# One-hot rows of the list positions on GpSimd, and the scaling of the later lists' one-hot rows on GpSimd

## The chip, the cores and the metric

One core of a Trainium2 chip. The time is the device time of one execution in microseconds (us). Before the change the kernel takes 706.0 us, the median of three runs (705.8 to 706.21).

## What is computed

Two steps, all in fp32 accuracy.

1. Attention with a window, for 8 batches and 8 heads of dimension 64: 512 local tokens see the 32 global keys and the local keys within 32 positions; the 32 global tokens see all 544 keys.
2. A mixture of eight experts on the 8 x 544 = 4352 result rows of 512 features. The choice is "sticky": a token takes its own best expert, or keeps that of the token ahead of it.

```python
for b in range(B):
    prev_e = -1
    for s in range(S):
        fresh_e = int(np.argmax(logits[b, s]))
        if s == 0 or local_gate[b, s] < 0.5: e = fresh_e
        else: e = prev_e if prev_e >= 0 else fresh_e
        prev_e = e
        ...
        h = np.maximum(x[b, s] @ w1[e], 0.0)
        out[b, s] = p[e] * (h @ w2[e])
```

Which tokens an expert gets depends on the data, so the kernel must sort the tokens by expert while it runs, and it does that with one-hot matmuls.

## The kernel before

**Stages.** The attention runs over 48 units (per batch four pairs of heads for the local tokens, two for the global ones). TensorE makes scores, transposes and products; VectorE takes maxima and divides; ScalarE takes exponentials and copies out of PSUM; GpSimd copies q and k into padded layouts (`prep`, line 191, six pieces a unit, two buffers). The result rows go to a table `xs` in device memory. Then the expert part runs in blocks: three early blocks of 256 tokens (`early`), which use only the tokens of batches 0 to 4, then eight blocks of each expert's rest (`rem`, one of ten code paths by a count), then full blocks. Each block does mm1 (line 1251, 8 groups of 12 matmuls), the ReLU on ScalarE (1253) and its low part on VectorE (1254), mm2 (1262), and a store by an indirect DMA from GpSimd (1268). Weights come in fp32 and are split into a high and a low part: ScalarE casts (1150), VectorE subtracts (1160, 128 x 1024 from SBUF to SBUF).

**The sorting.** For each of the 34 columns of 128 tokens the rank of a token in its expert's list is split into a low part `plo` (0 to 127) and a high part `phi`. `low` (line 905) builds a one-hot of the low part, `o1[:, c, :]`, 128 wide for each token column; `pick` builds the one-hot of the high part against the wanted chunks (line 989), and from it two scaled copies: times the column number `t1` (991) and times the partition number (993). A matmul of both, summed over the columns (999), gives in PSUM for each list place the number of its token, and VectorE makes the index from it (1001, 1002). Three picks are made:

- *early lists* (columns 0 to 20, in the attention), for blocks 0 to 2;
- *first later list* (`lists`, all 34 columns, four chunks wide), for block 3. Before it `low` builds the last 13 columns. It is made in block 2's mm1, and block 3's four gathers wait for its index;
- *other later lists* (`rest`, 54 chunks wide, in four groups of 9, 9, 8 and 8 columns), for everything after block 3. It is made in block 2's mm2; its o2 lies in the space of the tile `xT`, so the profile calls it xT. Its matmuls come at the end of block 2.

**What sets the order.** Every engine works in the order in which the code was written; there is no scheduler. The routing is a generator of small steps. In the attention `drip` takes steps from it at fixed places (a step that yields HEAVY ends the turn at that place); in the expert blocks `hook`, which is called after each of 24 places of a block, takes one. `every(g, n)` lets n steps through at a time. In the last block of the early ones, tokens of block 3 are transposed after mm2 steps 2, 4, 5 and 6 (line 1205, two PSUM banks in turn), copied high by ScalarE (1207) and low by VectorE (1208), which frees the bank.

Of the kernel before, what the change touches and what calls it, by code (L numbers as in the profile page):

```python
# [8 lines left out]
F32 = mybir.dt.float32  # L9
F32R = mybir.dt.float32r  # L10
BF16 = mybir.dt.bfloat16
I32 = mybir.dt.int32
AF = mybir.ActivationFunctionType
ALU = mybir.AluOpType
# [4 lines left out]
P = 128  # L19
# [4 lines left out]
E = 8  # L24
# [6 lines left out]
NT = 34  # L31
# [7 lines left out]
NX = 3  # L39
LISTS = "lists"  # L40
KINDS = "kinds"
HEAVY = "heavy"
NF = (B * S) // 256
NR = NF - NX - 1
# [9 lines left out]
LATE = 99  # L54
# [14 lines left out]
def lag(n):  # L69
    for _ in range(n):  # L70
        yield
# [495 lines left out]
class Consts:  # L567
# [17 lines left out]
    def rest(self):  # L585
        v = self.idf.rearrange("p (h e) -> p e h", h=4)
        self.nc.vector.tensor_reduce(out=self.sel, in_=v[:, 0:9], axis=AX.X, op=ALU.add)


class Route:  # L590
# [4 lines left out]
    def setup(self):  # L595
        nc, cst, c = self.nc, self.cst, self.pool
# [31 lines left out]
        self.rv = c.tile([P, E, CA], F32, name="rv")  # L628
        self.pos = c.tile([P, NT], F32, name="pos")
        self.pi = c.tile([P, 2, NT], I32, name="pi")  # L630
        self.plo = c.tile([P, NT], BF16, name="plo")
        self.o1 = c.tile([P, NT, P], BF16, name="o1")
        self.oe = c.tile([P, CA, 2, 2 * NX], BF16, name="oe")
        self.idx = c.tile([P, 2 * NX + 4 * E + 2 * NR], I32, name="idx")
# [56 lines left out]
        for g in range(4):  # L691
# [17 lines left out]
                                in1=self.io8.rearrange("p (e o) -> p e o", o=1).broadcast_to([P, E, E]), op=ALU.is_equal)  # L709
# [191 lines left out]
        yield  # L901

    def low(self, c0, c1):
        b1 = [P, c1 - c0, P]
        self.nc.vector.tensor_tensor(out=self.o1[:, c0:c1], in0=self.io128.rearrange("p (o k) -> p o k", o=1).broadcast_to(b1),
                                     in1=self.plo[:, c0:c1].rearrange("p (t o) -> p t o", o=1).broadcast_to(b1), op=ALU.is_equal)
        yield HEAVY

    def place(self, cntp, n, k0, nk):
        nc = self.nc  # L910
# [66 lines left out]
        yield  # L977
        yield from self.pick(cid, phi, self.oe, 0, 2 * NX, 0, ((0, CA),), po)

    def pick(self, cid, phi, o2, c0, c1, i0, groups, po, wait=2):  # L980
        nc = self.nc
        w = c1 - c0
        ci = cid.rearrange("p (o s) j -> p o (s j)", o=1)
        last = groups[-1][1]
        for t0, t1 in groups:
            ts = slice(t0, t1)
            b2 = [P, t1 - t0, w]
            e = o2[:, ts, 1, c0:c1]
            nc.vector.tensor_tensor(out=e, in0=ci[:, :, c0:c1].broadcast_to(b2), in1=phi[:, ts].rearrange("p (t o) -> p t o", o=1).broadcast_to(b2), op=ALU.is_equal)  # L989
            yield  # L990
            nc.vector.tensor_tensor(out=o2[:, ts, 0, c0:c1], in0=e, in1=self.t1[:, ts].rearrange("p (t o) -> p t o", o=1).broadcast_to(b2), op=ALU.mult)  # L991
            yield
            nc.vector.tensor_scalar(out=e, in0=e, scalar1=self.ipf, scalar2=None, op0=ALU.mult)
            yield
        yield from lag(wait)
        yield PSUM
        lp = po()
        for t in range(last):
            nc.tensor.matmul(lp[:, 0:2 * w], self.o1[:, t], o2[:, t, :, c0:c1], start=(t == 0), stop=(t == last - 1))  # L999
        l1 = self.tmp("l1", [P, 4 * E + 2 * NR], F32)[:, 0:w]  # L1000
        nc.vector.tensor_scalar(out=l1, in0=lp[:, 0:w], scalar1=float(P), scalar2=None, op0=ALU.mult)
        nc.vector.tensor_tensor(out=self.idx[:, i0 + c0:i0 + c1], in0=l1, in1=lp[:, w:2 * w], op=ALU.add)
        yield
# [61 lines left out]
        yield  # L1065

    def rest(self, po):
        yield from self.pick(*self.pk, self.o2, 4, 2 * (2 * E + NR), 2 * NX, ((0, 9), (9, 18), (18, 26), (26, NT)), po, LATE)


class Moe:
# [497 lines left out]
```

## Time and profile before

| what | value |
|---|---|
| runs | 705.8, 706.0, 706.21 us |
| profiled execution | 705.68 us, of which the span from first to last instruction is 704.0 |
| TensorE busy | 673.2 us, 96% of the span |
| VectorE busy | 428.2 us, 61% |
| GpSimd busy | 197.7 us, 28% |
| mean granted TensorE clock | 0.985 |

The profile gives one execution. Its timeline rows hold the start in us from the span's start, the length, the engine (PE is TensorE, PEld its weight load, DVE VectorE, ACT ScalarE, POOL GpSimd, SP the queue of the plain DMAs), the line of the kernel, the operation, what it writes and reads, and, in brackets, how long the engine was idle before it and what ended that. An xN at the end joins N neighbours. The attention lasts until about 240 us, the three early blocks until about 326, with the two later picks from 291 to 327, and the remaining blocks until the end.

### The profile page before, as it was taken

Reading aid. Unit: us, or ns where it says so; the run is one execution under the profiler, and the core shown is the slowest. Engines: PE = TensorE matmul, PEld = TensorE weight load, DVE = VectorE, ACT = ScalarE, POOL = GpSimd, SP = SyncE. Lnnn points to the kernel's source line nnn. Section 1 sums busy time; section 2 is a strip of 40 time slices with the busy share of each in tenths; the row PEclk is TensorE's granted clock in tenths of the full one; section 3 lists DMA queues with packets and bytes.
Section 4 is the critical chain, followed back from the end, with each engine's and each line's share of the span. In section 5 each row is a group of like instructions: output and inputs, shape, how many; then the busy total and the mean of one; then the engine's idle time right before and its main releaser. Section 6 shows DMA issues by size and latency. Waiting matters only on the chain.

```text
span 704.0 us, 18381 instructions
## 1 busy us (share of the span) xinstructions
PE 673.2 (96%) x7253; PEld 564.2 (80%) x7253; DVE 428.2 (61%) x1057; ACT 343.3 (49%) x614; POOL 197.7 (28%) x321
## 2 busy tenths in 40 slices
PE   9999999999899899998998999999999999999991
PEld 7777777777677778887887988889988889899890
DVE  7878777777887787994516625335445325165551
ACT  4565555655355664652325635243535334256551
POOL 7634344243333311132022312040304020223312
PEclk9999999999999999999999999999999999999996
DMA  8966967865756487767319737255557245176561
GB/s 329 383 232 228 354 242 271 324 258 205 292 182 244 173 319 248 269 220 273 131 66 314 241 116 254 70 182 175 195 173 234 98 126 167 65 262 237 187 215 51
DMA packets 43011, 151.44 MB, mean 215 GB/s; under 512 B 7965, under 2 KB 9245, under 8 KB 38688
## 3 DMA queue, kind: packets, MB, share of 16 engines
q1 hardware_dynamic: 35536, 126.92, 50.5%
q0 software_dynamic: 6960, 21.90, 9.3%
q8 instruction: 77, 1.26, 0.7%
q14 instruction: 150, 1.23, 0.6%
q10 hardware_dynamic: 288, 0.13, 0.1%
HBM read 130.55 MB, written 19.69 MB: 213 GB/s over the span
## 4 chain that ended last, share of the span: by engine, by line
PE 59%; DVE 3%; issue 1%; ACT 0%; POOL 0%; DVEq 0%; POOLq 0%; ACTq 0%
PE ps L1262 28%; PE ps L1251 26%; PE ps L1205 3%; DVE wq L1160 1%; DVE wp L1160 0%; PE ps L1374 0%; DVE xT L991 0%; PE ps L999 0%; DVE xl L1160 0%; POOL xa L1191 0%; DVE xT L989 0%; DVE wp L1208 0%; PE ps L276 0%; DVE wq L1366 0%; DVE hh L1160 0%
## 5 line engine op out<-in xcount | busy, mean ns | idle before, releaser
L1268 POOL DMA_INDIRECT out_dram<-y,tk x39 | 40.7, 1042 | 317.9 <-ACT y L1267 297.8
L1262 PE MATMUL ps<-wp,wq 128*128 128x512 f32 x504 | 128.0, 401 | 0.9 <-ACT wq L1365 0.9
L1262 PEld LDWEIGHTS ps<-wp,wq 128*128 128x128 f32 x504 | 93.5, 190 | 20.6 <-ACT wq L1365 1.1
L1251 PE MATMUL ps<-wp,wp 128*128 128x256 f32 (+5 forms) x672 | 109.4, 323 | 0.0
L1251 PEld LDWEIGHTS ps<-wp,wp 128*128 128x128 f32 x672 | 103.8, 189 | 4.8
L1254 DVE SCALAR_TENSOR_TENSOR wq<-ps,wq 128x256 fp32r<-128x256 f32 (+5 forms) x80 | 41.7, 526 | 73.3 <-ACT wq L1253 70.7
L191 POOL TENSOR_SCALAR_AFFINE_SELECT qbd<-raw 64x512 f32<-64x512 f32 x62 | 44.6, 719 | 120.2 <-PE ps L243 100.8
L1208 DVE TENSOR_TENSOR wp<-ps,wp 128x512 fp32r<-128x512 f32 x40 | 27.5, 691 | 79.8 <-ACT wp L1207 79.8
L1253 ACT ACTIVATE wq<-ps 128x256 fp32r<-128x256 f32 (+5 forms) x80 | 37.2, 468 | 78.6 <-PE ps L1251 68.7
L243 PE MATMUL ps<-kx,qbd 128*64 128x128 f32 x1024 | 71.3, 281 | 1.8 <-issue 1.8
L1267 ACT ACTIVATE y<-ps,pp 128x512 f32<-128x512 f32 x39 | 26.9, 690 | 77.3 <-PE ps L1262 71.0
L243 PEld LDWEIGHTS ps<-kx,qbd 128*64 128x64 f32 x1024 | 55.2, 138 | 11.7 <-issue 7.6
L248 DVE TENSOR_REDUCE mx<-ps 128x4 f32<-128x512 f32 x64 | 43.9, 686 | 28.5 <-PE ps L243 28.3
L1160 DVE TENSOR_TENSOR wp<-raw,wp 128x1024 fp32r<-128x1024 f32 x47 | 57.0, 1217 | 2.9 <-ACT wp L1150 2.8
L1191 POOL DMA_INDIRECT xa<-xs,idx x42 | 52.2, 1242 | 17.1 <-issue 10.0
L254 ACT ACTIVATE pe<-pe 128x512 f32<-128x512 f32 x64 | 40.7, 636 | 32.3 <-DVE pe L250 32.3
L1150 ACT CAST wp<-raw 128x1024 fp32r<-128x1024 f32 x49 | 50.8, 1046 | 1.5 <-DMA raw<-in_w_dram 0.7
L1207 ACT CAST wp<-ps 128x512 fp32r<-128x512 f32 x40 | 23.5, 591 | 55.1 <-PE ps L1205 55.1
L250 DVE TENSOR_TENSOR pe<-ps,mx 128x512 f32<-128x512 f32 x64 | 44.1, 688 | 1.6
L276 PE MATMUL ps<-v,pt 128*32 128x65 f32 x2048 | 43.1, 224 | 1.6 <-ACT pe L254 0.6
L276 PEld LDWEIGHTS ps<-v,pt 128*32 128x32 f32 x2048 | 33.7, 111 | 13.1 <-issue 7.5
L191 POOL TENSOR_SCALAR_AFFINE_SELECT kx<-raw 128x384 f32<-128x384 f32 (+3 forms) x127 | 43.1, 372 | 2.9 <-DMA raw<-in_qk_dram 0.8
(279 smaller groups left out, 1172.4 us busy)
## 6 DMA issues: line engine op xcount, KB each, us to landing
raw<-in_w_dram SPq DMA_DIRECT2D x78, 512.0 KB, 3.8
v<-in_vw_dram SPq DMA_DIRECT2D x32, 1040.0 KB, 9.8
raw<-in_qk_dram SPq DMA_DIRECT2D x32, 528.0 KB, 9.4
xa<-in_w_dram SPq DMA_DIRECT2D x26, 512.0 KB, 4.7
xT<-in_w_dram SPq DMA_DIRECT2D x20, 512.0 KB, 4.2
xs<-xa SPq DMA_DIRECT2D x8, 1056.0 KB
qgb<-in_qg_dram SPq DMA_DIRECT2D x8, 128.0 KB
xa<-xs,idx POOLq DMA_INDIRECT x42
```

The lines of the kernel that those rows point to most:

```text
L191: self.nc.gpsimd.affine_select(out=out, in_=in_, pattern=pat, compare_op=ALU.is_ge, fill=0.0, base=0, channel_multiplier=0)
L243: nc.tensor.matmul(sp[64 * t2:64 * t2 + 64, t], qbd[:, w], kf[:, f:f + P], start=False, stop=True, skip_group_check=True)
L248: nc.vector.tensor_reduce(out=mx, in_=st["sp"], axis=AX.X, op=ALU.max)
L250: nc.vector.tensor_tensor(out=st["pe"][:, 4 * hb:4 * hb + 4], in0=st["sp"], in1=mx.broadcast_to([P, 4, P]), op=ALU.subtract)
L254: self.nc.scalar.activation(out=pe, in_=pe, func=AF.Exp, scale=SCALE)
L276: nc.tensor.matmul(o[32 * w4:32 * w4 + 32, g, h], pt[:, 2 * g + w4 // 2, w4 % 2, h, :], v[:, w, h * (D + 1):(h + 1) * (D + 1)], start=True ...
L1150: nc.scalar.copy(out=hi, in_=raw)
L1160: (nc.gpsimd if pool else nc.vector).tensor_tensor(out=lo, in0=raw, in1=hi.bitcast(F32), op=ALU.subtract)
L1191: self.nc.gpsimd.indirect_dma_start(out=self.xr[j] if k == "early" else self.xr4[:, j], out_offset=None, in_=src, in_offset=bass.IndirectO ...
L1251: nc.tensor.matmul(ph, a[:, dc, fs], b_[:, dc, n0:n1], start=(n == 0), stop=(n == 11))
L1254: nc.vector.scalar_tensor_tensor(out=hl[:, fc, n0:n1], in0=ph, scalar=0.0, in1=hh[:, fc, n0:n1].bitcast(F32), op0=ALU.max, op1=ALU.subtract)
L1262: nc.tensor.matmul(py, a[:, fc, js], b_[:, fs], start=(fc == 0 and k == 0), stop=(fc == 7 and k == 2))
```

## The change

`low` no longer builds three or five columns with one VectorE comparison, but one column after the other with a GpSimd `tensor_scalar`, which compares the row 0 to 127 with one number per partition. For that `plo` is held in fp32. Its step no longer ends the turn of `drip`. In `rest`, and there alone, the two scalings of `pick` go to GpSimd.

```diff
-        self.plo = c.tile([P, NT], BF16, name="plo")
+        self.plo = c.tile([P, NT], F32, name="plo")
...
     def low(self, c0, c1):
-        b1 = [P, c1 - c0, P]
-        self.nc.vector.tensor_tensor(out=self.o1[:, c0:c1], in0=self.io128.rearrange("p (o k) -> p o k", o=1).broadcast_to(b1),
-                                     in1=self.plo[:, c0:c1].rearrange("p (t o) -> p t o", o=1).broadcast_to(b1), op=ALU.is_equal)
-        yield HEAVY
+        for c in range(c0, c1):
+            self.nc.gpsimd.tensor_scalar(out=self.o1[:, c], in0=self.io128, scalar1=self.plo[:, c:c + 1], scalar2=None, op0=ALU.is_equal)
+        yield
...
-    def pick(self, cid, phi, o2, c0, c1, i0, groups, po, wait=2):
+    def pick(self, cid, phi, o2, c0, c1, i0, groups, po, wait=2, share=False):
...
-            nc.vector.tensor_tensor(out=o2[:, ts, 0, c0:c1], in0=e, in1=self.t1[:, ts].rearrange("p (t o) -> p t o", o=1).broadcast_to(b2), op=ALU.mult)
+            eng = nc.gpsimd if share else nc.vector
+            eng.tensor_tensor(out=o2[:, ts, 0, c0:c1], in0=e, in1=self.t1[:, ts].rearrange("p (t o) -> p t o", o=1).broadcast_to(b2), op=ALU.mult)
             yield
-            nc.vector.tensor_scalar(out=e, in0=e, scalar1=self.ipf, scalar2=None, op0=ALU.mult)
+            eng.tensor_scalar(out=e, in0=e, scalar1=self.ipf, scalar2=None, op0=ALU.mult)
             yield
...
     def rest(self, po):
-        yield from self.pick(*self.pk, self.o2, 4, 2 * (2 * E + NR), 2 * NX, ((0, 9), (9, 18), (18, 26), (26, NT)), po, LATE)
+        yield from self.pick(*self.pk, self.o2, 4, 2 * (2 * E + NR), 2 * NX, ((0, 9), (9, 18), (18, 26), (26, NT)), po, LATE, True)
```

The lines after `low` move up by one, so that line 989 of before is 988 in the changed kernel; 991, 993 and 999 keep their numbers.

GpSimd's instructions in the attention, where the early lists are made (o_290 is `o1`, io the row 0 to 127; kx and qbd are the padded k and q). Before:

```order
L191 AFFINE_SELECT kx_146<-raw_79 128x32
L191 AFFINE_SELECT kx_146<-raw_79 128x7x32
L191 AFFINE_SELECT qbd_145<-raw_80 64x16x32 x2
L191 AFFINE_SELECT kx_147<-raw_80 128x128
L191 AFFINE_SELECT kx_147<-raw_80 128x6x64
```

Now:

```order
L191 AFFINE_SELECT kx_146<-raw_79 128x32
L191 AFFINE_SELECT kx_146<-raw_79 128x7x32
L905 TENSOR_SCALAR o_290<-io_261,plo 128x128 x21
L191 AFFINE_SELECT qbd_145<-raw_80 64x16x32 x2
L191 AFFINE_SELECT kx_147<-raw_80 128x128
L191 AFFINE_SELECT kx_147<-raw_80 128x6x64
```

All 21 columns stand ahead of one preparation of q and k; the routing steps behind them come up to a unit earlier on VectorE.

GpSimd's instructions in the early blocks (the four stores are those of blocks 0 and 1, xa receives block 3's tokens, cnd are the counts that choose the code path). Before:

```order
L1268 DMA out_dram<-y_4316,tk_95 4352x512
L1268 DMA out_dram<-y_4317,tk_95 4352x512
L1268 DMA out_dram<-y_4318,tk_96 4352x512
L1268 DMA out_dram<-y_4316,tk_96 4352x512
L1191 DMA xa_108<-xs,idx 128x528 x4
L1434 TENSOR_LOAD cnd
```

Now:

```order
L1268 DMA out_dram<-y_4331,tk_95 4352x512
L905 TENSOR_SCALAR o_290<-io_261,plo 128x128 x13
L1268 DMA out_dram<-y_4332,tk_96 4352x512
L1268 DMA out_dram<-y_4330,tk_96 4352x512
L1191 DMA xa_108<-xs,idx 128x528 x4
L991 TENSOR_TENSOR xT<-xT,t_264 128x9x54
L993 TENSOR_SCALAR xT<-xT,ipf 128x9x54
L991 TENSOR_TENSOR xT<-xT,t_264 128x9x54
L993 TENSOR_SCALAR xT<-xT,ipf 128x9x54
L991 TENSOR_TENSOR xT<-xT,t_264 128x8x54
L993 TENSOR_SCALAR xT<-xT,ipf 128x8x54
L1434 TENSOR_LOAD cnd
```

The 13 columns stand between the stores of blocks 0 and 1, the scalings behind the gathers; the fourth pair comes behind the read of the counts.

VectorE's instructions in block 2's mm2, where the later lists are made. Before:

```order
L989 TENSOR_TENSOR xT<-cid,phi 128x9x54
L991 TENSOR_TENSOR xT<-xT,t_264 128x9x54
L993 TENSOR_SCALAR xT<-xT,ipf 128x9x54
L989 TENSOR_TENSOR xT<-cid,phi 128x9x54
L1160 TENSOR_TENSOR wp_4208<-raw_79,wp_4208 128x1024
L991 TENSOR_TENSOR xT<-xT,t_264 128x9x54
L993 TENSOR_SCALAR xT<-xT,ipf 128x9x54
L989 TENSOR_TENSOR xT<-cid,phi 128x8x54
```

Now:

```order
L988 TENSOR_TENSOR xT<-cid,phi 128x9x54 x2
L1160 TENSOR_TENSOR wp_4222<-raw_79,wp_4222 128x1024
L988 TENSOR_TENSOR xT<-cid,phi 128x8x54 x2
L1160 TENSOR_TENSOR wp_4326<-raw_80,wp_4326 128x1024
L1434 TENSOR_LOAD cnd
```

The eight scalings have left VectorE's queue; the weight subtractions (1160) follow the comparisons directly, and behind them stands the first L1208.

## The prediction

> **What bounds the kernel now.** I read the page first, then a table of stretches, then TensorE's and VectorE's timelines around the two places that the change touches.
>
> The page's first part (engine, busy time, share of the span, instructions) says that TensorE is the bound:
>
> ```profile
> PE 673.2 (96%) x7253; PEld 564.2 (80%) x7253; DVE 428.2 (61%) x1057; ACT 343.3 (49%) x614; POOL 197.7 (28%) x321
> ```
>
> VectorE at 61% would not matter on average, so the stretches decide. The table gives, for each, its length, then each engine's busy time, the granted TensorE clock, the DMA share and GB/s:
>
> ```profile
> 189.00:197.00 8.00, 6.39 (x94) 4.53 (x97) 4.76 (x21) 2.17 (x6) 2.79 (x6) 0.79 0.32 130
> 295.00:307.00 12.00, 12.00 (x126) 11.77 (x125) 10.87 (x27) 5.75 (x11) 5.72 (x5) 1.00 0.73 232
> 318.00:327.00 9.00, 6.84 (x54) 5.51 (x54) 5.46 (x11) 2.45 (x4) 1.00 (x1) 0.81 0.59 198
> ```
>
> From 295 to 307 TensorE is full and VectorE is busy 10.87 of 12 us: it follows at its heels. From 318 to 327 TensorE loses 2.16 us outright, and the clock stands at 0.81 (of 9 us, 0.19 x 9 = 1.7 us of work lost). TensorE's timeline (start, length, what, idle before and its releaser) shows why:
>
> ```profile
> 318.29 0.39 PE L1262 MATMUL ps<-wq,hl 128*128 128x512 f32 x1
> 320.84 1.03 PE L1205 MATMUL ps<-idf,xa 128*128 128x128 f32 x4 [2.16 <-DVE wp L1208]
> ```
>
> The third transpose of block 3's tokens waits for a PSUM bank that VectorE's first L1208 must empty, and that L1208 comes late because VectorE first works off the later lists:
>
> ```profile
> 309.44 0.64 DVE L989 TENSOR_TENSOR xT<-cid,phi 128x486 bf16<-128x486 bf16 x1
> 310.12 0.67 DVE L991 TENSOR_TENSOR xT<-xT,t 128x486 bf16<-128x486 bf16 x1
> 310.82 0.36 DVE L993 TENSOR_SCALAR xT<-xT,ipf 128x486 bf16<-128x486 bf16 x1
> ...
> 318.97 1.22 DVE L1160 TENSOR_TENSOR xl<-raw,xh 128x1024 fp32r<-128x1024 f32 x1
> 320.10 1.28 DVE L1208 TENSOR_TENSOR wp<-ps,wp 128x512 fp32r<-128x512 f32 x2
> ```
>
> **The question of the port.** Taking work from VectorE helps only if GpSimd can do it beside VectorE. These rows say that it can't (VectorE and GpSimd, two places):
>
> ```profile
> 231.88 2.97 DVE L740 TENSOR_TENSOR lvm<-sk,lvm 128x5 f32<-128x5 f32 x1
> ```
> ```profile
> 232.43 2.38 POOL L1160 TENSOR_TENSOR wp<-raw,wp 128x1024 fp32r<-128x1024 f32 x1
> ```
> ```profile
> 56.41 1.33 POOL L191 TENSOR_SCALAR_AFFINE_SELECT kx<-raw 128x128 f32<-128x128 f32 x4
> ```
> ```profile
> 203.05 1.52 POOL L191 TENSOR_SCALAR_AFFINE_SELECT kx<-raw 128x128 f32<-128x128 f32 x4
> ```
> ```profile
> 56.67 0.57 DVE L760 TENSOR_SCALAR lsu<-lsu 128x5 f32<-128x5 f32 x1
> ```
> ```profile
> 203.02 0.33 DVE L925 TENSOR_TENSOR hb<-oh,bs 128x168 f32<-128x168 bf16 x1
> ```
> ```profile
> L760 DVE TENSOR_SCALAR lsu<-lsu x8: 172/370/567, 56.7 to 271.2; 128x5 f32<-128x5 f32 x8
> ```
>
> L740 subtracts five columns and ends at 234.85, 0.04 us after GpSimd's subtraction. L760 takes 172 ns alone and 0.57 us when it starts in a run of four GpSimd pieces; it ends at 57.24, before the run does (57.74), so it got in between two pieces. The other way round, GpSimd's same run takes 1.52 us where L925, with both inputs in SBUF, stands at its start. So I treat them as one server for work from SBUF to SBUF: whoever is in finishes his instruction, then the one who waits goes. VectorE's operations on PSUM (L1254, L1208) I leave out of it. The Trainium skill (SBUF — State Buffer, Who interferes with whom) speaks against the change: a VectorE instruction with two SBUF inputs and a GpSimd instruction that reads SBUF exclude each other for the whole instruction. By that rule the sum is the one below, and without it the first rival's; the rows agree with it for L740 and L925, while for L1160 against GpSimd no row shows it.
>
> **Prices.** The trace has no compare and no scaling on GpSimd. The nearest rows (shape, count, total us, mean ns):
>
> ```profile
> L191 POOL TENSOR_SCALAR_AFFINE_SELECT kx<-raw 128x384 f32<-128x384 f32 x32 | 17.5, 547 | 0.0
> ...
> L191 POOL TENSOR_SCALAR_AFFINE_SELECT kx<-raw 128x128 f32<-128x128 f32 x32 | 9.9, 310 | 2.9 <-DMA raw<-in_qk_dram 0.8
> L191 POOL TENSOR_SCALAR_AFFINE_SELECT kx<-raw 128x32 f32<-128x32 f32 x32 | 6.8, 214 | 0.0
> ...
> L1160 POOL TENSOR_TENSOR wp<-raw,wp 128x1024 fp32r<-128x1024 f32 x2 | 4.8, 2378 | 4.4 <-DVE gx L774 4.4
> ```
>
> One column of 128 one-hots (one input): above 0.21 us (the 32-column piece), below 0.30 us (128 columns at the two-input rate of 2378/1024 = 2.32 ns). I take 0.28, a little under 0.31, since in the run at 56.41 the pieces overlap slightly. L991 (two inputs): 486 x 2.32 = 1.13 us and 1.00 for 432 columns, above; 486 x 547/384 = 0.69, below; I take 1.1 and 1.0, since the two-input row is the nearest in kind. L993 (one input): 214 + 454 x (547 - 214)/352 ns = 0.64 us, between 0.36 (VectorE's own) and 1.13.
>
> **The sum, part by part.**
>
> *Lists of the first half (attention).* VectorE loses seven L905, GpSimd gains 21 pieces:
>
> ```profile
> L905 DVE TENSOR_TENSOR o<-io,plo 128x384 bf16<-128x384 bf16 x8 | 4.4, 553 | 0.0
> ```
> ```profile
> 190.96 1.51 POOL L191 TENSOR_SCALAR_AFFINE_SELECT qbd<-raw 64x512 f32<-64x512 f32 x2 [8.45 <-PE ps L243]
> ```
> ```profile
> 198.47 1.09 PE L243 MATMUL ps<-kx,qbd 128*64 128x128 f32 x16
> ...
> 205.10 0.44 PE L352 MATMUL ps<-idf,xa 128*128 128x128 f32 x2 [0.79 <-DVE xa L284]
> ```
>
> 21 x 0.28 = 5.9 us goes ahead of one preparation of q and k, in a GpSimd idle time of 8.45 us, and that preparation is first read at 198.47: hidden, and even at 0.30 it ends some 5 us early. VectorE's 7 x 0.55 = 3.9 us come out while TensorE is full; the routing steps that moved up fill the same slots earlier. At best the wait of 0.79 us on VectorE goes; at worst it comes back elsewhere with a piece of blocking. I take **-0.3** (-1.1 to +0.5).
>
> *Lists of the second half.* This is where the port bites. VectorE's timeline, and the matmuls on TensorE that read the one-hots:
>
> ```profile
> 291.41 1.22 DVE L1160 TENSOR_TENSOR wp<-raw,wp 128x1024 fp32r<-128x1024 f32 x1
> ...
> 292.74 1.55 DVE L905 TENSOR_TENSOR o<-io,plo 128x640 bf16<-128x640 bf16 x2
> 294.21 1.22 DVE L1160 TENSOR_TENSOR wq<-raw,wq 128x1024 fp32r<-128x1024 f32 x1
> 295.34 0.55 DVE L905 TENSOR_TENSOR o<-io,plo 128x384 bf16<-128x384 bf16 x1
> 295.81 0.29 DVE L989 TENSOR_TENSOR xT<-cid,phi 128x136 bf16<-128x136 bf16 x1
> ...
> 300.06 0.75 DVE L1254 SCALAR_TENSOR_TENSOR hl<-ps,hh 128x256 fp32r<-128x256 f32 x2
> ```
> ```profile
> 298.05 1.01 PE L999 MATMUL ps<-xT,o 128*128 128x8 bf16 x34
> ```
>
> Today the one-hots are built at 292.74 and 295.34 and L999 finds them ready at 298.05. Now 13 pieces start at 291.45; behind them on GpSimd stands only the store of block 1's first half, and its y is one of three buffers, not written again until block 2. Between 291.41 and the first L1254 VectorE still has ten SBUF operations (five L1160, L1029, L1031, L989, L991, L993): without L905, 8.65 - 1.47 - 0.47 = 6.7 us. If each lets one piece in, L1254 starts at 291.41 + 6.7 + 10 x 0.28 = 300.9, and only then, on operations that read PSUM, do the last three pieces run through: 301.8. L999 needs the last column; it ends at 302.0 instead of 299.06: **+3.0** (at 0.21 us: 2.2; pieces that all run first end at 295.1, but then L1254, at 300.06 - 1.94 + 3.64 = 301.8, holds up the fourth L1251 group by over 1 us). Behind L999 the index, the gathers and everything on TensorE move with it. Such a gap also lowers the clock: after the gaps at 189 and 318 the stretches stand at 0.79 and 0.81, 1.7 us each. Here TensorE still trickles; I add **+1.0** (0 to 1.7).
>
> *Later lists.* From the first L989 to the first L1208 VectorE now needs 320.10 - 309.44 = 10.66 us. Without the scaling it needs 4 x 0.60 + 4 x 1.13 + 0.1 = 7.0. But GpSimd's pieces come between its L1160 and L989: three L991 and three L993 by the time of L1208, some of the last one beside VectorE's read of the counts, 1.1 + 0.64 + 1.1 + 0.64 + 0.6 + 0.6 = 4.7. Sum 11.7, **+0.8** after the 0.2 us by which VectorE had lagged (-3.7 without any blocking, +2 with L993 at 1.13). The last pair ends about 1.5 us after L1208, when TensorE, at 2 x (0.44 + 0.7) us of transposes and matmuls, just gets to L999: hidden; with slower pieces it becomes the next wait.
>
> Sum: -0.3 + 3.0 + 1.0 + 0.8 = **+4.5 us**. The profiled execution took 705.68, so 710.2; the runs' median is 0.3 above it, so **710.5**.
>
> **Rivals.**
> 1. *The engines don't exclude each other here* (the bf16 operations or L1160 escape). Then the pieces are ready at 295.1, VectorE needs 7.0 us instead of 10.66, and the wait of 2.16 us goes with its slow clock: -0.3 - 2.2 - 1.7 = -4.2, **701.8**. For it: VectorE is the releaser at 320.84 and GpSimd is idle there. Against: the rows of the port. Chance 0.25.
> 2. *The pieces are so cheap that both places cancel*: no place in the rows goes that low. By the Trainium skill (GPSIMD Engine Reference, Performance versus the Vector engine) a one-input body runs at 1.03 cycles an element of 1.2 GHz, an estimate of 0.11 us a column and 0.42 for L993; then L999 waits some 0.5 us, VectorE's stretch hardly changes, and the time would be about 706.5. With pieces at half my price the same result follows from my schedule: 300.06 - 1.94 + 1.4 + 0.4 = 299.9, a wait of 0.9, against a gain of about 1.3 before L1208: **706**. Chance 0.08.
> 3. *Compare and scaling cost more than the copies* (0.45 us a column, scalings a third more): 13 pieces end at 304, the scalings after L1208: +8, **714**. Nothing in the trace excludes it. Chance 0.10.
> Forecast: 0.57; its own range 707.5 to 713.
>
> **How the numbers follow.** A difference under 0.2% (1.4 us) is no change. Forecast and third rival are slower: 0.67; the second is the same: 0.08; the first faster: 0.25. The range reaches down to the first rival with some gain in the attention, 700.5, and up to half of the third's, 713.5.
>
> **What would show it.** In the changed profile: L999 at about 298 with a wait for GpSimd of some 3 us, columns of 0.28 us stretched among VectorE's L1160; VectorE's L1160 above 1.22 us where a scaling precedes it; the third transpose still waiting for L1208. Wrong, if L1160 stays at 1.22 us beside running GpSimd pieces, if the 13 pieces end before 298, or if the 2.16 us wait has gone.

## The result and the profile after

The changed kernel takes 713.91 us (median of five runs, 711.45 to 715.45) against 706.0 for the kernel before (704.2 to 707.08 beside it): a ratio of 1.0109, with a 95% interval from 1.0088 to 1.0131. It is slower, as forecast, but by 7.7 us instead of 4.5, and just above the range (713.5). The profiled execution took 713.91 us, of which the span is 712.2. The page's first part says that TensorE still sets the time and that only GpSimd has more to do:

```profile
PE 676.8 (95%) x7253; PEld 566.5 (80%) x7253; DVE 420.6 (59%) x1039; ACT 343.1 (48%) x614; POOL 235.8 (33%) x363
```

GpSimd gained 235.8 - 197.7 = 38 us of busy time, VectorE lost 428.2 - 420.6 = 7.6. The 38 us are not all work: part of it is instructions that are counted as busy and don't get on. That shows where the 13 later columns stand. GpSimd's timeline of the changed kernel, column by column (start, length; the columns behind 297.63 are left out, each takes 0.59 us):

```profile
290.21 1.62 POOL L905 TENSOR_SCALAR o<-io,plo 128x128 bf16<-128x128 bf16 x1 [17.73 <-DVE cid L1026]
291.82 1.52 POOL L905 TENSOR_SCALAR o<-io,plo 128x128 bf16<-128x128 bf16 x1
293.33 0.65 POOL L905 TENSOR_SCALAR o<-io,plo 128x128 bf16<-128x128 bf16 x1
293.96 2.38 POOL L905 TENSOR_SCALAR o<-io,plo 128x128 bf16<-128x128 bf16 x1
296.32 1.33 POOL L905 TENSOR_SCALAR o<-io,plo 128x128 bf16<-128x128 bf16 x1
297.63 0.59 POOL L905 TENSOR_SCALAR o<-io,plo 128x128 bf16<-128x128 bf16 x1
...
```

VectorE in the same stretch:

```profile
290.10 1.22 DVE L1160 TENSOR_TENSOR wp<-raw,wp 128x1024 fp32r<-128x1024 f32 x1
...
291.53 1.21 DVE L1160 TENSOR_TENSOR wq<-raw,wq 128x1024 fp32r<-128x1024 f32 x1
...
293.50 2.45 DVE L1160 TENSOR_TENSOR wq<-raw,wq 128x1024 fp32r<-128x1024 f32 x2
295.87 1.30 DVE L1160 TENSOR_TENSOR wq<-xa,wq 128x1024 fp32r<-128x1024 f32 x1
```

A column costs 0.59 us when nothing is in its way (from 297.63 on). While VectorE works off its subtractions a column takes up to 2.38 us, and five are done by 297.65; the other eight come after VectorE's row has ended. VectorE pays little: a subtraction takes 1.21 to 1.30 us where it took 1.22 before. TensorE then waits for each of the last nine columns, and its clock falls (TensorE's timeline, then the table of stretches: length, busy time of PE, PEld, DVE, ACT and POOL, granted clock, DMA share, GB/s):

```profile
296.73 0.79 PE L999 MATMUL ps<-xT,o 128*128 128x8 bf16 x25
297.70 0.18 PE L999 MATMUL ps<-xT,o 128*128 128x8 bf16 x1 [0.19 <-POOL o L905]
...
302.32 0.19 PE L999 MATMUL ps<-xT,o 128*128 128x8 bf16 x1 [0.39 <-POOL o L905]
```
```profile
302.50:307.50 5.00, 5.00 (x25) 5.00 (x25) 1.74 (x4) 0.38 (x1) 3.92 (x4) 0.50 0.44 134
```

L999 ends at 302.51 instead of 299.06, though TensorE came to it 1.3 us earlier (296.73 against 298.05), so some 4.8 us are lost in it, and the next 5 us run at half the clock: 2.5 us of work are lost there.

At the other later lists the wait of 2.16 us for L1208 has gone, and another has come. GpSimd's scalings, and TensorE's matmuls that read them:

```profile
315.27 6.93 POOL L991 TENSOR_TENSOR xT<-xT,t 128x486 bf16<-128x486 bf16 x1 [4.71 <-DVE xT L988]
322.30 1.53 POOL L993 TENSOR_SCALAR xT<-xT,ipf 128x486 bf16<-128x486 bf16 x1
323.81 0.99 POOL L991 TENSOR_TENSOR xT<-xT,t 128x486 bf16<-128x486 bf16 x1
...
329.72 1.37 POOL L993 TENSOR_SCALAR xT<-xT,ipf 128x432 bf16<-128x432 bf16 x1
```
```profile
326.16 1.03 PE L999 MATMUL ps<-xT,o 128*128 128x108 bf16 x18
328.80 0.54 PE L999 MATMUL ps<-xT,o 128*128 128x108 bf16 x8 [1.61 <-POOL xT L993]
331.14 0.65 PE L999 MATMUL ps<-xT,o 128*128 128x108 bf16 x8 [1.80 <-POOL xT L993]
```

VectorE's row there begins and ends so, and between these rows it has no gap:

```profile
314.54 1.22 DVE L988 TENSOR_TENSOR xT<-cid,phi 128x486 bf16<-128x486 bf16 x2
...
320.13 1.21 DVE L1160 TENSOR_TENSOR xl<-raw,xh 128x1024 fp32r<-128x1024 f32 x1
322.15 0.69 DVE L1208 TENSOR_TENSOR wp<-ps,wp 128x512 fp32r<-128x512 f32 x1 [0.81 <-ACT wp L1207]
```

The first scaling stands for 6.93 us where its like takes 0.99, and ends 0.9 us after VectorE's row (321.34). The first L1208 waits for ScalarE and is no longer late.

### The profile page after: what moved, and what is told of

The parts are those of the page before. It is cut to its first block, busy times and chain, and to the rows that moved or that the text cites. A ratio compares the mean times of both kernels' runs of the same rounds, so it can differ in the third digit from the quotient of the medians.

```text
span 712.2 us, 18411 instructions
## 1 busy us (share of the span) xinstructions
PE 676.8 (95%) x7253; PEld 566.5 (80%) x7253; DVE 420.6 (59%) x1039; ACT 343.1 (48%) x614; POOL 235.8 (33%) x363
## 4 chain that ended last, share of the span: by engine, by line
PE 57%; DVE 4%; POOL 2%; issue 1%; DMA 0%; ACT 0%; POOLq 0%; DVEq 0%; SPq 0%; ACTq 0%
PE ps L1262 28%; PE ps L1251 25%; PE ps L1205 2%; DVE wp L1160 1%; POOL o L905 1%; DVE wq L1160 1%; DMA raw<-in_w_dram 0%; PE ps L1374 0%; DVE hl L1254 0%; POOL xa L1191 0%; DVE xl L1208 0%; POOL xT L993 0%; DVE xl L1160 0%; PE ps L276 0%; DVE hl L1160 0%
## 5 line engine op out<-in xcount | busy, mean ns | idle before, releaser
L1268 POOL DMA_INDIRECT out_dram<-y,tk x39 | 39.0, 999 | 281.8 <-ACT y L1267 272.8
L1262 PEld LDWEIGHTS ps<-wp,wq 128*128 128x128 f32 x504 | 94.1, 191 | 21.3 <-ACT wq L1365 1.3
L1254 DVE SCALAR_TENSOR_TENSOR wq<-ps,wq 128x256 fp32r<-128x256 f32 (+5 forms) x80 | 41.8, 525 | 75.8 <-ACT wq L1253 61.6
L1208 DVE TENSOR_TENSOR wp<-ps,wp 128x512 fp32r<-128x512 f32 x40 | 27.5, 691 | 80.6 <-ACT wp L1207 80.5
L243 PEld LDWEIGHTS ps<-kx,qbd 128*64 128x64 f32 x1024 | 55.4, 138 | 12.2 <-issue 8.5
L1160 DVE TENSOR_TENSOR wp<-raw,wp 128x1024 fp32r<-128x1024 f32 x47 | 56.8, 1215 | 2.8 <-ACT wp L1150 2.8
L262 ACT COPY pt<-ps 128x512 f32<-128x512 f32 x64 | 34.9, 610 | 18.9 <-PE ps L260 15.1
```

The source lines that it names most:

```text
L243: nc.tensor.matmul(sp[64 * t2:64 * t2 + 64, t], qbd[:, w], kf[:, f:f + P], start=False, stop=True, skip_group_check=True)
L1160: (nc.gpsimd if pool else nc.vector).tensor_tensor(out=lo, in0=raw, in1=hi.bitcast(F32), op=ALU.subtract)
L1254: nc.vector.scalar_tensor_tensor(out=hl[:, fc, n0:n1], in0=ph, scalar=0.0, in1=hh[:, fc, n0:n1].bitcast(F32), op0=ALU.max, op1=ALU.subtract)
L1262: nc.tensor.matmul(py, a[:, fc, js], b_[:, fs], start=(fc == 0 and k == 0), stop=(fc == 7 and k == 2))
```

## The experiments

The theory after the first comparison, V in the expectations: while VectorE has operations with two SBUF inputs ready one behind the other, GpSimd is held off, and gets in only now and then; and GpSimd's form with a scalar per partition is dearer than I took it. Its rival, A, is what the prediction used: the two take turns, one GpSimd piece at each end of a VectorE operation. Others are named with the runs. In the kernels of the experiments lines are shifted by a few: a column is L907, the list's matmul L1006 (L1011 and L1010 in the later ones), the subtraction L1167 (L1172, L1171), the low part of the transposes L1215 (L1220, L1219). Each ratio is to the kernel before, run beside it.

### One part of the change at a time

First half alone: the flag `share` stays false, and `low` builds the later columns on VectorE as before.

```diff
     def low(self, c0, c1):
+        if c0 < CA:
             for c in range(c0, c1):
                 self.nc.gpsimd.tensor_scalar(out=self.o1[:, c], in0=self.io128, scalar1=self.plo[:, c:c + 1], ...)
             yield
+            return
+        ...  # the VectorE comparison of before, from a bf16 copy of plo
```

> Only the 21 columns of the first half (attention) go to GpSimd; the 13 later columns and all scalings stay on VectorE. Theory V (at the later lists VectorE's two-input operations hold GpSimd off; the first half has no such place): TensorE ends the attention about 1.3 us earlier, as block 1's mm2 did in the changed kernel (293.85 against 295.17), and nothing else moves: 704.7 us. Theory D (a column is simply dear wherever it stands, 0.59 us, and delays the padded q and k behind it): not faster than 706.0.

Second half alone: the same with `c0 >= CA` (this kernel ran four times, from 706.37 to 713.08 us, and its profile is of the slowest).

> Only the 13 later columns go to GpSimd. Theory V: the 13 columns stretch over about 12 us as in the changed kernel, L999 ends 5 us later, the clock falls to about 0.8 for some 10 us: 712.5 us. If the scalings cost most of the 8 us (rival S): about 707.5, and then the run with the scalings alone stands at 712 or more.

Scalings alone: `low` as before, `share` as in the change.

> Only the eight scalings of the other later lists go to GpSimd. From the changed kernel, where the end of this L999 is late by no more (5.2 us) than the end of block 2's mm1 before it (5.4): the wait of 2.16 us for L1208 goes with its slow clock, and waits of 1.6 and 1.8 us for the scalings come at L999: 705.8 us (704.5 to 707). Rival S: 712 or more.

| part on GpSimd | ratio (95% interval) | in us of 706 |
|---|---|---|
| columns of the first half | 0.9965 (0.9947 to 0.9983) | -2.5 |
| 13 later columns | 1.0083 (1.0051 to 1.0115) | +5.9 |
| eight scalings | 1.0031 (1.0013 to 1.0048) | +2.2 |

The first half is a gain, of 2.5 us where I expected 1.3; the two others are losses, and the 13 columns are the largest part. The sum is +5.6 us against +7.7 for the whole; the intervals of the parts add up to more than that difference, so no interaction is shown. Rival S (the scalings cost most) and rival D (a column is dear wherever it stands) have fallen.

With the second half alone the clock falls as in the full change. The table of stretches of that run, right behind its list's matmul:

```profile
306.00:311.00 5.00, 4.90 (x24) 4.91 (x25) 1.46 (x4) 0.38 (x1) 3.92 (x5) 0.50 0.40 128
```

With the scalings alone, the same 6.93 us stand as in the full change, and the two waits again; TensorE's timeline and the table of stretches:

```profile
320.81 0.54 PE L1006 MATMUL ps<-xT,o 128*128 128x108 bf16 x8 [1.75 <-POOL xT L1000]
323.15 0.88 PE L1006 MATMUL ps<-xT,o 128*128 128x108 bf16 x8 [1.80 <-POOL xT L1000]
```
```profile
318.00:325.00 7.00, 3.45 (x38) 2.88 (x38) 1.87 (x6) 0.78 (x2) 6.33 (x7) 0.76 0.64 223
325.00:338.00 13.00, 13.00 (x54) 11.07 (x53) 3.68 (x5) 4.16 (x6) 4.47 (x5) 0.87 0.63 212
```

One wait of about 2.1 us was traded for two of 1.8, and from the first of them on the clock stands at 0.76 and 0.87. In this profile that is where the time goes, and not into a late L1208. My expectation of 705.8 (0.9997) missed: it had the waits and left out the clock behind them.

### Is it the second SBUF input?

As the second half alone, but four of the five subtractions beside the columns become a reduction over one element, which reads one tile (the kernel leaves out those four subtractions, so the low parts of four pieces of weights hold a copy of the high part):

```diff
-            nc.vector.tensor_tensor(out=lo, in0=raw, in1=hi.bitcast(F32), op=ALU.subtract)
+            if self.one:      # block 1, the end of mm2
+                ...
+                    nc.vector.tensor_reduce(out=lo, in_=hi.bitcast(F32).rearrange("p (n o) -> p n o", o=1), axis=AX.X, op=ALU.add)
+            else:
+                ...           # the subtraction as before
```

> As the run with the 13 later columns alone on GpSimd, but four of the five subtractions L1160 that VectorE runs beside them read one SBUF tile instead of two: they copy the high part (a reduction over one element, same size, same place, after the same cast), so the low parts of four pieces of weights are wrong and the numbers with them. Theory V (two SBUF inputs on VectorE hold GpSimd off): from the second subtraction on a column takes 0.59 us, the last one ends near 300 instead of near 303, L999 waits 1 to 2 us instead of 5, and the run takes about 708 us. Rival P (GpSimd is slow there for a reason of its own, say its instructions come late, or it loses to any VectorE work): the columns stretch over 12 us again and the time is that of the run with the second half alone, about 712.5.

The ratio is 1.0027 (1.0008 to 1.0047). VectorE's timeline shows the same row, with reductions of the same length as the subtractions:

```profile
290.37 1.22 DVE L1172 TENSOR_TENSOR wp<-raw,wp 128x1024 fp32r<-128x1024 f32 x1
...
291.80 1.21 DVE L1170 TENSOR_REDUCE wq<-wq 128x1024 fp32r<-128x1024 f32 x1
...
294.18 3.46 DVE L1170 TENSOR_REDUCE wq<-wq 128x1024 fp32r<-128x1024 f32 x3
```

And GpSimd runs through, but for the first column, which starts beside the one subtraction that still has two inputs (two of the 13 and the last):

```profile
290.49 1.62 POOL L907 TENSOR_SCALAR o<-io,plo 128x128 bf16<-128x128 bf16 x1 [17.68 <-DVE cid L1033]
292.10 0.60 POOL L907 TENSOR_SCALAR o<-io,plo 128x128 bf16<-128x128 bf16 x1
...
298.46 0.59 POOL L907 TENSOR_SCALAR o<-io,plo 128x128 bf16<-128x128 bf16 x1
```

The last column ends at 299.05, 8.56 us after the first began, against 12.06 with the subtractions as they are. So GpSimd is not held off because VectorE is busy, and not by a lateness of its own: rival P has fallen. It is the two-input subtraction that holds it off; the run changes the number of inputs and the kind of instruction together, so that it is the inputs and not the kind is not shown by it. The Trainium skill (SBUF — State Buffer, Who interferes with whom) says that it is the inputs: a VectorE instruction with one SBUF input, outside the modes that use two ports, leaves GpSimd alone, and one with two does not. The trace agrees: 0.59 us beside the one, up to 2.38 beside the other. Two short operations that VectorE has between the reductions, L998 and L1000, pay instead: 0.53 and 0.46 us where they took 0.30 and 0.28.

What the subtractions cost by holding GpSimd off is 1.0083 - 1.0027, about 4 us, with intervals that leave room for some 1.5 to 6.5. The remaining 1.9 us stand beside a list's matmul that ends 1.3 us late (it waits 0.40 us for each of the last two columns) and a clock of 1.00 behind it.

### Do the two engines take turns?

As the second half alone, with four of the five subtractions cut into four pieces:

```diff
+            if self.one:      # the same four
+                for j in range(0, 1024, 256):
+                    c = slice(j, j + 256)
+                    nc.vector.tensor_tensor(out=lo[:, c], in0=raw[:, c], in1=hi[:, c].bitcast(F32), op=ALU.subtract)
+            else:
+                ...           # the subtraction as before
```

> As the run with the 13 later columns alone on GpSimd, but four of the five subtractions L1160 that VectorE runs beside them are each cut into four pieces of 256 columns, so that VectorE has 12 more ends of an operation in that row; the computation is the same. Theory A (the prediction's: at each end of a VectorE operation the waiting GpSimd instruction goes, then VectorE again): all 13 columns get in during the row, each piece behind a column starts up to 0.59 us late, the row grows from 7.0 us to 12 us or more, and L999 does not wait for the columns one by one. Theory G (operations of one kind that stand ready back to back leave no room; GpSimd gets in only where VectorE has a gap, at a change of operation or where it waits for its own result): 4 or 5 columns by the end of the row as before, the row grows by the fixed part of the pieces alone (under 1.5 us), and then 8 or 9 columns come one each 0.58 us with L999 waiting for each: ratio 1.008 to 1.012.

The ratio is 1.0083 (1.0066 to 1.0101), and neither theory has it right. VectorE's row, and GpSimd's columns beside it:

```profile
293.91 3.06 DVE L1171 TENSOR_TENSOR wq<-raw,wq 128x256 fp32r<-128x256 f32 x8
296.89 1.51 DVE L1171 TENSOR_TENSOR wq<-xa,wq 128x256 fp32r<-128x256 f32 x4
```
```profile
294.37 1.12 POOL L907 TENSOR_SCALAR o<-io,plo 128x128 bf16<-128x128 bf16 x1
...
297.67 1.12 POOL L907 TENSOR_SCALAR o<-io,plo 128x128 bf16<-128x128 bf16 x1
```

More columns get in than before (eight end by 298.79, not five), so an end between two ready operations of one kind does let GpSimd in, against theory G. But it is one column for each 1.12 us, that is for three pieces of 0.38 us and not for each, and no piece behind a column is 0.59 us late: the row grew by 1.1 us in all, against theory A. The last five columns come after the row, and the list's matmul waits for each; behind it the clock is 0.50 for 5 us, as with whole subtractions. What decides which end lets GpSimd in is open. In the full change the scaling at 315.27 was let in at none of the six ends ahead of the row's own.

### Who pays when GpSimd is in

Two runs change the form and the share of the scalings. In both the first half's columns are on GpSimd and the later 13 on VectorE.

```diff
-            eng.tensor_scalar(out=e, in0=e, scalar1=self.ipf, scalar2=None, op0=ALU.mult)
...                            # on GpSimd:
+                eng.tensor_tensor(out=e, in0=e, in1=self.ipb.rearrange("p (t o) -> p t o", o=1).broadcast_to(b2), op=ALU.mult)
```

All four groups on GpSimd:

> The first half's columns and all eight scalings of the other later lists on GpSimd, the 13 later columns on VectorE; the second scaling of each group multiplies by a tensor (the partition number held in bf16) instead of a scalar per partition. Theory F (the form sets GpSimd's price: 2.6 ns an element with a scalar, 1.5 with a second tensor): the scaling that took 1.37 to 1.53 us takes 0.91 to 0.99, the waits of L999 for GpSimd shrink from 1.75 and 1.80 us to about 1 each or less, and the time is that of the first half alone within 1 us (ratio to before 0.995 to 0.998). If the second scaling is slow for its place (both read and written in the same tile), it stays at 1.4 to 1.5 us, the two waits stay, and the ratio is about 1.000 (0.9965 + 0.0031).

The first two groups only (`eng = nc.gpsimd if share and t0 < 18 else nc.vector`):

> As the run before, but only the scalings of the first two of the four groups go to GpSimd. Theory V (GpSimd's first scaling starts to move only when VectorE's row of two-input operations ends) : VectorE's L1208 comes 2 us earlier than with all scalings on VectorE, so the wait of about 2.1 us at the third transpose is nearly gone, the four GpSimd scalings take 4 us from the end of VectorE's row, and L999 waits for them by under 1 us: ratio 0.993 to 0.996, the fastest so far. If GpSimd's operations get in between VectorE's after all, L1208 is late by up to 2 us again and the ratio is that of the first half alone, 0.9965, or above.

With all four the ratio is 0.9960 (0.9942 to 0.9979), within what was expected. The second scaling takes 0.91 to 1.00 us where it took 1.37 to 1.53, so it is the form (a bf16 tensor in place of a scalar per partition), as theory F has it. The first scaling stands for 6.93 us as before. Against the first half alone (0.9965) the eight scalings in this form show neither gain nor loss. The waits of L999 shrink, the second only to 1.49 us where I expected about 1:

```profile
316.93 1.00 POOL L1003 TENSOR_TENSOR xT<-xT,ipb 128x486 bf16<-128x486 bf16 x1
```
```profile
321.87 0.54 PE L1011 MATMUL ps<-xT,o 128*128 128x108 bf16 x8 [0.45 <-POOL xT L1003]
323.90 0.54 PE L1011 MATMUL ps<-xT,o 128*128 128x108 bf16 x8 [1.49 <-POOL xT L1003]
```

With two groups it is 0.9997 (0.9979 to 1.0016), and that is a miss. GpSimd's first scaling, and VectorE's timeline there:

```profile
308.23 3.01 POOL L1000 TENSOR_TENSOR xT<-xT,t 128x486 bf16<-128x486 bf16 x1 [3.03 <-DVE xT L997]
```
```profile
310.40 1.29 DVE L1000 TENSOR_TENSOR xT<-xT,t 128x432 bf16<-128x432 bf16 x1
311.73 0.95 DVE L1005 TENSOR_SCALAR xT<-xT,ipf 128x432 bf16<-128x432 bf16 x1
312.61 1.40 DVE L997 TENSOR_TENSOR xT<-cid,phi 128x432 bf16<-128x432 bf16 x1
313.93 2.02 DVE L1172 TENSOR_TENSOR wp<-raw,wp 128x1024 fp32r<-128x1024 f32 x1
```
```profile
319.86 1.11 PE L1217 MATMUL ps<-idf,xa 128*128 128x128 f32 x4 [3.28 <-DVE wp L1220]
```

Here something like the turns of my prediction does appear. VectorE's L1000 needs the result of the comparison before it, and there GpSimd's first scaling gets in (it ends at 311.24, as L1000 is held up). From then on VectorE's operations take 1.29, 0.95, 1.40 and 2.02 us where they took 0.61, 0.33, 0.60 and 1.22 in the kernel before. That the wait of L1000 for its input is what lets GpSimd in is my reading of this one place; no run tests it. The transpose waits 3.28 us for L1208, worse than the 2.16 before, and the clock from 316 to 326 is 0.66.

### The rest

The first half with the step that ends the turn (`yield HEAVY` behind the columns):

> As the run with the first half alone on GpSimd, but the step of the columns still ends the turn of the attention's side work, as before the change, so that the columns come as 15 and 6 and the routing behind them stands later. If the gain of the first half comes from VectorE's 3.9 us: 0.9965 again (0.995 to 0.998). If it comes from the routing steps that moved up: about 1.000.

Ratio 0.9982 (0.9968 to 0.9997), between the two values that I had named: a gain remains when the routing steps stay where they were. Whether their earlier place adds to it can't be told from intervals that overlap.

The kernel before once more:

> The kernel before, unchanged, profiled beside these runs: ratio 1.000 within 0.002. The wait of 2.16 us at the third transpose should stand again (2.0 to 2.2), and the clock in the 9 us behind it should show whether 0.81 belongs to that wait (as I took it) or not: with the first half alone the wait of 2.05 stood there with a clock of 1.00.

Ratio 1.0004 (0.9981 to 1.0026). Its wait of 2.20 us at the third transpose stands where 2.16 stood, and the clock of the 9 us around it is 0.81 again. Length of wait and clock still don't go together over all runs: 2.05 us was followed by 1.00 (first half alone), 2.16 and 2.20 by 0.81, 3.28 by 0.66 (two groups), and in the run with the turn ended a wait of 2.99 by 1.00 (TensorE's timeline and the table of stretches of that run):

```profile
318.90 0.65 PE L1212 MATMUL ps<-idf,xa 128*128 128x128 f32 x4 [2.99 <-DVE wp L1215]
```
```profile
318.00:327.00 9.00, 7.04 (x61) 6.02 (x62) 3.58 (x10) 1.86 (x4) 3.08 (x4) 1.00 0.72 233
```

A scaling on ScalarE:

```diff
+                nc.scalar.mul(out=o2[:, ts, 1, c0:c1], in_=e, mul=self.ipf)      # e is o2[:, ts, 0, c0:c1] here
...
             eng.tensor_tensor(out=o2[:, ts, 0, c0:c1], in0=e, ...)      # eng is GpSimd
```

> First half's columns on GpSimd, the 13 later columns on VectorE; of the two scalings of each group the one by the partition number goes to ScalarE (a multiplication by a scalar per partition, ahead of the other one, from the unscaled rows) and the one by the column number to GpSimd. Theory V: GpSimd's four operations of 0.91 to 1.0 us begin to move when VectorE's row ends, at about 316, and are through 4 us later, as TensorE gets to L999: no wait for them beyond 0.5 us, none at the third transpose, the clock stays at 1.00 behind: ratio 0.991 to 0.994. If ScalarE's four extra operations delay its casts and the copies of the transposes (L1150, L1207), the transposes wait for these instead: 0.996 or above.

Ratio 0.9994 (0.9974 to 1.0014), a miss. VectorE's and TensorE's timelines:

```profile
311.28 1.23 DVE L1171 TENSOR_TENSOR wp<-raw,wp 128x1024 fp32r<-128x1024 f32 x1 [1.14 <-ACT wp L1161]
```
```profile
316.15 0.66 PE L1216 MATMUL ps<-idf,xa 128*128 128x128 f32 x4 [2.02 <-DVE wp L1219]
...
323.43 16.79 PE L1262 MATMUL ps<-wp,wp 128*128 128x480 f32 x63 [3.15 <-issue]
```

ScalarE works in order too: its casts stood behind scalings that waited for VectorE's comparisons, VectorE then waited for the casts, and L1208 (L1219 here) was late by 2.02 us again. No matmul of the list waits for GpSimd any more; but ahead of block 3 TensorE then waits 3.15 us for something that the profile does not name, where it was about 1 us or less in other runs. That stays open.

The first half alone once more, in five rounds:

> The first half's columns alone on GpSimd once more, beside the run before and in more rounds: ratio 0.9965 (0.995 to 0.998), TensorE busy 22.3 to 22.9 us from 176 to 200 (19.6 to 21.3 with the columns on VectorE).

Ratio 0.9964 (0.9946 to 0.9981), TensorE busy 22.30 us from 176 to 200. It beats both kernels: 700.72 us beside 703.31 for the kernel before.

## Why the prediction was wrong in size

The direction came out, for the reason given (L999 waits for the columns), and the number did not. By the prediction's own terms:

| term | predicted, us | measured, us |
|---|---|---|
| lists of the first half | -0.3 | -2.5 |
| lists of the second half and the clock | +3.0 and +1.0 | +5.9 |
| later lists | +0.8 | +2.2 |
| sum of the parts | +4.5 | +5.6 |
| whole change | +4.5 | +7.7 |

Two steps of the second half's term failed, one in the mechanism and one in the size.

**The mechanism failed at "if each lets one piece in".** I had read the rows of the port as one server that serves by turns. L740 and L925 showed that the engines get in each other's way, which holds. They did not show turns. Ten ends of an operation should have let ten columns in, and VectorE was to pay 0.28 us for each. Five got in. L1254 starts at 297.10 where it was 300.06; 1.3 us of that are the earlier arrival and 1.9 the comparisons that are gone, so the columns held VectorE up by some 0.3 us in all, not 2.8. The columns in turn were later than I had them. One of my own rows spoke against turns, had I looked ahead of it:

```profile
231.46 0.95 POOL L1191 DMA_INDIRECT xr<-xs,idx  x1 [3.52 <-PE ps L243]
```

L740 starts at 231.88, takes 0.16 us elsewhere (the median of its eight), and GpSimd's subtraction begins only at 232.43, as this instruction ends. L740 was there first and still ended behind the subtraction. What held it until 232.43 the profile does not name, but the end of a GpSimd instruction did not let it in.

**The size failed at the price of a column, 0.28 us against 0.59 measured;** L993, 0.64, was less than half of 1.37 to 1.53. I had bounded a column from above by 0.30, the two-input rate, on the ground that one input can't cost more than two. It can: 486 elements take 1.53 us with a scalar per partition and 0.99 with a second tensor. The price carries the miss in L999, and the turns pulled the other way: turns at 0.59 us would have put the last column, by the prediction's own schedule, at about 291.4 + 6.7 + 13 x 0.59 = 305.8, and it ended at 302.3 with a start 1.3 us earlier. So the two errors partly cancelled. (A slip beside it: at 0.21 us the same schedule gives +2.0 and not +2.2.)

The third rival, with 0.45 us a column and the scalings a third more, gives 714, the time that came. It was right that the scalings end behind L1208, but its 714 is in part luck: its price is still too low, and it keeps the turns. Beside one-input operations the same columns cost 1.9 us, not 5.9.

**The clock, +1.0 of a range of 0 to 1.7, was 2.5 us:** 5 us at 0.50 behind L999. I took it low because TensorE "still trickles" there. It does, 0.18 us in 0.58, and that did not keep the clock up. The Trainium skill (TensorE: Matmul & The Clock Gate, What's actually happening) has a clock that is either full or half and is decided over windows of about 3.4 us that run freely. The row at exactly 0.50 agrees with the half clock; that waits of 2.05 to 2.99 us were followed now by 1.00 and now by 0.81 agrees with windows that don't start with the wait.

**Later lists: the term was right in sign and wrong in its way.** I had GpSimd's scalings come between VectorE's operations, and L1208 late. GpSimd got in nowhere (6.93 us), VectorE's row took 6.8 us, L1208 came in time, and the 2.16 us wait went, one of the signs that I had named against myself. A second one, L1160 at 1.22 us beside running pieces, nearly came (1.21 to 1.30). In place of the late L1208 came the wait that I had called hidden, at L999, as "slower pieces" would have it.

**First half: the sign came out, and the ground for the size was wrong.** I wrote that VectorE's 3.9 us come out "while TensorE is full". It was not full there, and my first table said so: from 189 to 197 TensorE is busy 6.39 of 8 us, at a clock of 0.79. I used that gap for the clock and put it at nothing here. The table of stretches, of the kernel before (profiled again) and of the first half alone:

```profile
176.00:200.00 24.00, 19.57 (x334) 13.47 (x338) 18.23 (x65) 8.25 (x20) 6.88 (x15) 0.86 0.57 217
```
```profile
176.00:200.00 24.00, 22.44 (x475) 16.18 (x475) 19.48 (x82) 11.88 (x29) 19.48 (x38) 1.00 0.61 227
```

Over these 24 us TensorE is busy 19.6 to 21.3 us in the six profiles with the 21 columns on VectorE, at clocks of 0.86 to 1.00, and 22.3 to 22.8 in the seven with the columns on GpSimd, always at 1.00. Most of the difference is one gap. TensorE and VectorE in the first profile of before:

```profile
190.61 0.27 PE L243 MATMUL ps<-kx,qbd 128*64 128x128 f32 x1 [1.84 <-issue]
```
```profile
190.92 0.69 DVE L248 TENSOR_REDUCE mx<-ps 128x4 f32<-128x512 f32 x1 [1.94 <-PE ps L243]
```

TensorE stands for 1.84 us, the profile names nothing that it waits for, and VectorE stands idle beside it. The gap is 1.0 to 2.9 us in all six profiles with the columns on VectorE, 0.2 in the run with the turn ended, and absent in the other six. So the gain goes with the columns, but not simply through a VectorE that is busy at that moment; what the gap waits for is open. The 21 columns took 12.2 us, not 5.9, and did reach the padded q and k: in the first half alone TensorE waits 0.60 us for them once, so "some 5 us early" was wrong, at a small price.

**First rival (the engines don't exclude each other):** fallen, by the columns of up to 2.38 us beside the subtractions. **Second (so cheap that both places cancel):** fallen, by the price. From the Trainium skill (GPSIMD Engine Reference, Performance versus the Vector engine) came the estimate of 0.11 us a column and 0.42 for L993; the trace has 0.59 and 1.37 to 1.53, and the measurement decides.

In the full change's profile there is a further loss of some 2 us behind block 3 (where the code path changes TensorE waits 1.00 us, 0.27 before, and the clock of the 24.5 us from 378.5 on is 0.86, 0.93 in the like stretch before). One profile shows it; its cause wasn't looked for.

## What to carry to other kernels

In this kernel, work moved from VectorE to GpSimd lost where VectorE had a row of operations with two SBUF inputs ready: there most of GpSimd's work came when the row had ended, or VectorE paid for letting it in. So look at what VectorE does in the stretch in which the moved work must be finished, not at its share of busy time, and move only the parts whose consumer comes late; here the first part of the change alone is 0.35% faster than the kernel before and the whole is 1.1% slower. And price a form by a row of the same form: one input was not cheaper than two.

## What the runs showed that I had not expected

- On GpSimd a bf16 multiplication of 128 x 486 takes 1.53 us with a scalar per partition and 0.99 us with a second tensor; a comparison of 128 x 128 with a scalar takes 0.59 us.
- A GpSimd instruction that waits for its turn counts as busy: 6.93 us for 0.99 us of work. GpSimd's busy time rose by 38 us for about 30 us of work at the free prices (34 columns of 0.59 us, four pairs of scalings of 2.3 to 2.5 us).
- What VectorE pays differs from place to place. A column that got in cost its subtraction 0.1 us; the scalings with two inputs that got in cost each of four VectorE operations 0.6 to 0.8 us.
- Nine waits, eight of them of 0.4 us, with 0.18 us of work between them were followed by 5 us at a clock of 0.50, and a single wait of 2.99 us by a clock of 1.00.
